# The first unit's probabilities leave PSUM once, as float32, and TensorE multiplies them with the natural values

## The chip, the cores and the metric

The kernel runs on one core of one Trainium2 chip. The metric is the device time of one execution in microseconds (us). The five engines are named as in the profile: PE (TensorE, matrix products; PEld is its weight load), DVE (VectorE), ACT (ScalarE), POOL (GpSimd) and SP (SyncE, which here issues the DMAs). A float32 is exact to 24 bits and a float16 to 11, so this kernel carries most operands as a pair of float16: a high half, and a low half that holds what the high half lost. A product of two such pairs is then three matmuls: high by high, high by low, low by high.

## The reference: clustered attention, then a two-layer network

Inputs: `q`, `k`, `v` of shape (4, 8, 768, 64), that is batch, heads, sequence and head size; 16 centroids per head; weights `w_in` (512 x 2048) and `w_out` (2048 x 512). All are float32.

```python
q_assign = np.argmax(np.einsum('bhsd,hcd->bhsc', q_n, c_n), axis=-1)
k_assign = np.argmax(np.einsum('bhsd,hcd->bhsc', k_n, c_n), axis=-1)
mask = q_assign[:, :, :, None] == k_assign[:, :, None, :]
scores = scale * np.matmul(q, k.transpose(0, 1, 3, 2))
scores = np.where(mask, scores, -1000000000.0)
scores = scores - np.max(scores, axis=-1, keepdims=True)
attn = np.exp(scores)
attn = attn / (np.sum(attn, axis=-1, keepdims=True) + 1e-09)
return np.matmul(attn, v)
```

A query sees only the keys that have the same nearest centroid. The result, as a (3072 x 512) matrix x, goes through `h = x @ w_in`, through a function g (h where h >= 1, 0 where h <= -1, (h + 1)^2 / 4 between), and through `g @ w_out`.

## The kernel before, in words

**Units.** The work is cut into 12 units: four batches (`b`), each in three chunks (`c`) of 256 queries. The heads are taken in four pairs (`hp`). A unit therefore has 16 softmax tiles: four head pairs, two heads (`j`), two tiles of 128 queries (`t`). Each tile is 128 queries by 768 keys.

**One tile.** `at_scores` (lines 891 to 920) multiplies q and k into one of two PSUM pairs (`pair`, two banks each), four matmuls of 384 columns, and DVE copies the scores to an `sS` buffer with their row minimum. `at_soft` (lines 922 to 956) takes the exponential on ACT, with the row sum. The products with v need the probabilities transposed, in `pT`, and there are two ways to that. In all units but the first, ACT writes the high half to an `hl` buffer (three of them), POOL subtracts for the low half, and a DMA transposes both into `pT` (line 955). In the first unit (`by_tensor`, line 958) TensorE transposes six blocks of the float32 probabilities back into the PSUM pair, ACT copies the high half out (line 945), TensorE subtracts that half from the pair with minus the identity `idm` (line 948), and ACT copies what is left, the low half (line 949). In this way the pair is held from the scores to the second copy.

**The products with v.** `at_av` (lines 972 to 1007) spreads the reciprocals of the row sums with 8 small matmuls, then does 36 matmuls per head pair: 6 key blocks, three products of halves, two heads side by side in one bank (`bank_a`). The weights are 64 columns of v, the moving operand 256 columns of `pT`. DVE multiplies the result with the reciprocals into `xn`, and ACT and POOL split it into halves for the network.

**K and V of a head pair** lie in one slot of three parts (`kv_load`, line 668): k arrives in part 1, v in part 2. `k_split` writes the transposed k into part 0. `v_split` (line 709) scales v by a power of two `sv` and writes its halves into part 1, where k had been. `k_assign` finds the clusters of the keys and writes their transposed marks `k1` into part 2, where v had been; so `k1` has to wait for `v_split`, and the scores need `k1`. The scale comes from `v_bound` (line 594, a DVE reduction for each head pair, `v_am` in the profile) and `batch_scale` (line 616), for the whole batch.

**The weights of the network** are scaled and split during the first unit and a part of the second: for each of 16 blocks `w_bits` (ACT and DVE) and `w_split` (two ACT passes, one POOL pass).

**The order of the work** is written by a planner in the kernel (`Recorder`, lines 49 to 322). Each call is recorded with a step number; step 0 is the first score tile, each softmax tile is one step, a unit 16. A model of costs turns the record into one order for each engine, over 80 rounds, and keeps the best; the step numbers are only the first round's priorities. All recorded instructions are issued at line 322, and so nearly every row of the profile has that line. For the first batch `v_split` is entered 6.5 steps ahead of its head pair's first tile (line 1203). A change of the recorded work lets the planner write the whole order anew. Line 102 books a matmul with a float32 moving operand as four times its columns.

Of the kernel before, what the change touches and what calls it, by code (L numbers as in the profile page):

```python
# [24 lines left out]
UNIT = 2.0**-10  # L25
# [394 lines left out]
class Ring:  # L420
# [4 lines left out]

    def __call__(self, *shape, dtype):
        self.i += 1
        return view(self.bufs[self.i % len(self.bufs)], shape, dtype)


def view(buf, shape, dtype):
# [13 lines left out]
def tile_clustered_attention_moe(  # L445
# [33 lines left out]
    PRO = -14  # L479
    FA = SC + LA  # L480
    EARLY = 22
    WA, WR = -4, 2.2

    RAW = [3, 4, 5, 6, 7, 4, 5, 6, 0, 7, 6, 7, 0, 7, 0, None]
# [62 lines left out]
    idb = idf.bitcast(BF16).rearrange("p (q a) -> p q a", a=2)[:, :, 1]  # L547
    idu = const.tile([P, P], F16, name="idu")
    rec.gpsimd.tensor_scalar(out=idu, in0=idf, scalar1=UNIT, scalar2=None, op0=ALU.mult)
    idm = const.tile([P, P], F16, name="idm")  # L550
    rec.gpsimd.tensor_scalar(out=idm, in0=idf, scalar1=-1.0, scalar2=None, op0=ALU.mult)
    iota = const.tile([P, C], F32, name="iota")
    for c in range(C):
        nc.gpsimd.memset(iota[:, c : c + 1], float(C - c))
# [61 lines left out]
    def batch_scale(b):  # L616

        e = BX[b]
        ar = misc(NP + 1)
        rec.tensor.matmul(ar[:, :NP], ones, e["am"], start=True, stop=True)  # L620
        mx = ar[:, NP:]
        isx, sv = new("isx", [1], F32, 3), new("sv", [1], F32, 3)
        rec.vector.tensor_reduce(out=mx, in_=ar[:, :NP], op=ALU.max, axis=AX.X)
        to_scale(mx, sv)
        rec.vector.tensor_copy(isx, mx)
        e.update(isx=isx, sv=sv)

    def transpose(out, nat, ps=None):
        nat = nat.rearrange("p n a d -> p (n a d)")
# [78 lines left out]

    def v_split(b, hp):
        e = KV[b, hp]  # L710
        vs = e["vs"] = view(e["parts"][1], [2, 2, T * D], F16)
        split(vs[:, 0], vs[:, 1], e["v"], BX[b]["sv"])

    def k_assign(b, hp):

        e = KV[b, hp]
        n = 2 * T
        z1 = misc(n, C)
        kn = e["kn"]
        mx = labels(z1, e["kT"], n, [2 * hp + i // T for i in range(n)])  # L720
        rec.vector.tensor_tensor(out=z1, in0=z1, in1=mx, op=ALU.subtract)
        rec.gpsimd.memset(kn[:, :, 1, C:], 0.0)
        rec.vector.tensor_scalar(
            out=kn[:, :, 1, :C], in0=z1, scalar1=0.0, scalar2=-ONE, op0=ALU.not_equal, op1=ALU.mult
        )
        e["k1"] = view(e["parts"][2], [n, P], F16)
        transpose(e["k1"], kn, pair[start()] if b == hp == 0 else None)

        pn = misc(2, C)
        with rec.group():  # L730
            for t in range(T):
                rec.tensor.matmul(pn, ones, kn[:, t::T, 1, :C], start=(t == 0), stop=(t == T - 1))
        rec.vector.tensor_scalar(
            out=BX[b]["has"][:, hp], in0=pn, scalar1=-ONE * (S - 0.5), scalar2=None, op0=ALU.is_gt
        )
# [186 lines left out]
    def at_soft(b, hp, c, j, t):  # L922
        e = A.setdefault((b, hp, c), {})
        n = j * CT + t
        sS, bi, pS = A.pop((b, hp, c, j, t))
        if n == 0:
            e["rs"] = new("rs", [4], F32, 4)
        if t == 0:
            e["pT", j] = new("pT", [2 * T, CT, P], F16, 3)
        sf = sS.rearrange("p a s -> p (a s)")  # L930
        rec.scalar.activation(
            out=sf, in_=sf, func=AF.Exp, bias=bi, scale=-1.0, accum_out=e["rs"][:, n : n + 1]
        )
        pT = e["pT", j]
        if by_tensor(b, hp, c, j, t):
            with rec.group():
                for i in range(T):
                    to = pS[:, i // 3, i % 3 * P : (i % 3 + 1) * P]
                    rec.tensor.matmul(
                        to, sf[:, i * P : (i + 1) * P], idf, start=(i % 3 == 0), stop=False, is_transpose=True,  # L940
                        skip_group_check=True,
                    )
            pt = pS[:, :, :HS].rearrange("p h (n q) -> p h n q", q=P)
            hi, lo = (pT[:, x * T : (x + 1) * T, t, :].rearrange("p (h n) q -> p h n q", h=2) for x in range(2))
            rec.scalar.copy(hi, pt)
            with rec.group():
                for h in range(2):
                    rec.tensor.matmul(pS[:, h, :HS], idm, hi[:, h], start=False, stop=True, skip_group_check=True)
            rec.scalar.copy(lo, pt)
            at_sums(e, n)  # L950
            return
        hl = new("hl", [2, S], F16, 3)
        rec.scalar.copy(hl[:, 0], sf)
        rec.gpsimd.tensor_tensor(out=hl[:, 1], in0=sf, in1=hl[:, 0], op=ALU.subtract)
        rec.sync.dma_start_transpose(out=pT[:, :, t, :], in_=hl.rearrange("p a s -> p (a s)"))
        at_sums(e, n)

    def by_tensor(b, hp, c, j, t):

        return early() and b == c == 0  # L960

    def at_sums(e, n):
        if n == 3:
# [8 lines left out]
    def at_av(b, hp, c):  # L972
        u = b * NCH + c
        e, kv = A.pop((b, hp, c)), KV[b, hp]

        pv, rb = bank_a[:, :CQ], bank_a[:, CQ:]
        with rec.group():
            for t in range(CT):
                for a in range(2):
                    for j in range(2):  # L980
                        n = j * CT + t
                        rec.tensor.matmul(
                            rb[j * D : (j + 1) * D, t * P : (t + 1) * P],
                            e["rr"][:, a, n : n + 1].to_broadcast([P, D]),
                            idu,
                            start=(a == 0),
                            stop=(a == 1),
                        )
            for kc in range(T):
                for i, (va, pa) in enumerate(((0, 0), (0, 1), (1, 0))):  # L990
                    for j in range(2):
                        pT = e["pT", j].rearrange("p (a n) t q -> p a n (t q)", a=2)[:, pa, kc]
                        rec.tensor.matmul(
                            pv[j * D : (j + 1) * D],
                            kv["vs"][:, va, j, kc * D : (kc + 1) * D],
                            pT,
                            start=(kc == 0 and i == 0),
                            stop=(kc == T - 1 and i == 2),
                        )
        rs = new("rb", [CQ], F32)  # L1000
        rec.scalar.copy(rs, rb)
        xn = rs
        rec.vector.tensor_tensor(out=xn, in0=pv, in1=rs, op=ALU.mult)
        if hp == 0:
            X[u] = new("x", [2, NP, CQ], F16)
        rec.scalar.copy(X[u][:, 0, hp], xn)
        rec.gpsimd.tensor_tensor(out=X[u][:, 1, hp], in0=xn, in1=X[u][:, 0, hp], op=ALU.subtract)
# [190 lines left out]
    for b in range(B):  # L1198
        for hp in range(NP):
            s0 = first(b, hp, 0)  # L1200

            if b == 0:
                steps = [PRO, s0 - 9, s0 - 8, s0 - 6.5, s0 - 6]
            else:
                steps = [first(b - 1, hp, NCH - 1) + SC + LA - 3] + [s0 - x for x in (6, 5.6, 5, 4)]
            for x, fn in zip(steps, (kv_load, k_scale, k_split, v_split, k_assign)):
# [74 lines left out]
```

## Time and profile before

| | |
|---|---|
| timed runs, median of 3 | 872.43 us (872.41 to 873.12) |
| profiled execution, span from first to last instruction | 870.7 us |
| PE busy | 812.9 us (93%) |
| DVE busy | 647.3 us (74%) |
| ACT busy | 650.3 us (75%) |
| POOL busy | 546.3 us (63%) |
| mean granted clock of PE | 0.983 |

The span is the time that the profile shows of the profiled execution; what lies around it is not in the trace, and the median of the timed runs is 1.7 us above it. The engines' shares are means over the whole span. The first 180 us or so differ from the rest, and so the profile has to be read by stages. In a row of a group stand the line, the engine, the operation, output <- inputs, the shapes and the count; then busy time and the mean of one in ns; then idle time of the engine just before, and what ended it.

### The profile page before, as it was taken

Reading aid. Unit: us, or ns where it says so; the run is one execution under the profiler, and the core shown is the slowest. Engines: PE = TensorE matmul, PEld = TensorE weight load, DVE = VectorE, ACT = ScalarE, POOL = GpSimd, SP = SyncE. Lnnn points to the kernel's source line nnn. Section 1 sums busy time; section 2 is a strip of 40 time slices with the busy share of each in tenths; the row PEclk is TensorE's granted clock in tenths of the full one; section 3 lists DMA queues with packets and bytes.
Section 4 is the critical chain, followed back from the end, with each engine's and each line's share of the span. In section 5 each row is a group of like instructions: output and inputs, shape, how many; then the busy total and the mean of one; then the engine's idle time right before and its main releaser. Section 6 shows DMA issues by size and latency. Waiting matters only on the chain.

```text
span 870.7 us, 19881 instructions
## 1 busy us (share of the span) xinstructions
PE 812.9 (93%) x7532; PEld 566.1 (65%) x7532; DVE 647.3 (74%) x1535; ACT 650.3 (75%) x1144; POOL 546.3 (63%) x528
## 2 busy tenths in 40 slices
PE   3677768999999999999999999999999999999998
PEld 3454546667667767767767766767766666766664
DVE  7999999989878777668789848867687758444322
ACT  6999998798777688777767777787777787776232
POOL 1245499797655768756757677766757667766222
PEclk9888899999999999999999999999999999999999
DMA  9956689779999979989999969989898797766100
GB/s 315 241 180 164 164 206 200 140 123 194 169 186 197 183 146 179 190 152 164 195 177 188 176 126 178 188 158 179 168 202 178 145 174 127 127 116 110 20 25 25
DMA packets 404193, 141.01 MB, mean 162 GB/s; under 512 B 372736, under 2 KB 396288, under 8 KB 404096
## 3 DMA queue, kind: packets, MB, share of 16 engines
q1 hardware_dynamic: 404096, 139.73, 81.2%
q8 instruction: 59, 0.97, 0.5%
q14 instruction: 38, 0.31, 0.1%
HBM read 40.40 MB, written 6.29 MB: 54 GB/s over the span
## 4 chain that ended last, share of the span: by engine, by line
PE 76%; DVE 10%; ACT 7%; issue 3%; POOL 2%; DMA 2%; SPq 0%; ACTq 0%; POOLq 0%; DVEq 0%
PE pair L322 37%; PE banka L322 11%; PE bankh L322 9%; PE banki L322 9%; PE bankj L322 9%; POOL hl L322 2%; DVE sS L322 2%; ACT sS L322 1%; ACT w L322 1%; DVE w L322 1%; ACT pT L322 1%; DVE r L322 1%; DVE qn L322 1%; DMA kv<-in_v_dram 1%; ACT hl L322 1%
## 5 line engine op out<-in xcount | busy, mean ns | idle before, releaser
L322 POOL TENSOR_TENSOR hl<-sS,hl 128x768 f16<-128x768 f32 x176 | 298.9, 1703 | 111.5 <-ACT hl L322 86.7
L322 PE MATMUL pair<-w,g 128*128 128x512 f16 x1152 | 271.1, 379 | 0.3 <-ACT o L322 0.3
L322 PEld LDWEIGHTS <-w 128*128 128x128 f16 x2304 | 223.2, 98 | 48.6 <-issue 7.1
L322 ACT ACTIVATE sS<-sS,sbi 128x768 f32<-128x768 f32 x192 | 179.4, 934 | 85.7 <-DVE sbi L322 75.7
L322 DVE CUSTOM_DVE_ANT_0 sS<-pair,zero,er 128x768 f32<-128x768 f32 x192 | 194.1, 1011 | 61.4 <-PE pair L322 47.7
L322 PEld LDWEIGHTS <-g 128*128 128x128 f16 x1152 | 110.2, 98 | 116.1 <-issue 2.9
L322 PE MATMUL pair<-kv,q 128*128 128x384 f16 x768 | 159.1, 331 | 20.2 <-ACT pT L322 9.1
L322 POOL TENSOR_TENSOR g<-r,g 128x512 f16<-128x512 f32 x88 | 106.0, 1204 | 72.2 <-ACT g L322 68.5
L322 ACT CAST hl<-sS 128x768 f16<-128x768 f32 x176 | 144.1, 827 | 4.3 <-DMA pT<-hl 2.5
L322 PEld LDWEIGHTS <-q 128*128 128x128 f16 x1152 | 83.9, 98 | 76.3 <-issue 28.9
L322 PEld LDWEIGHTS <-kv 128*64 128x64 f16 (+1 forms) x2112 | 104.5, 108 | 5.8 <-issue 1.9
L322 ACT ACTIVATE r<-r,f_ra,f_rs 128x512 f32<-128x512 f32 x88 | 71.5, 812 | 45.3 <-DVE r L322 42.8
L322 PE MATMUL banka<-pT,kv 128*64 128x256 f16 x1728 | 103.6, 274 | 1.7 <-DMA pT<-hl 1.7
L322 ACT CAST g<-r 128x512 f16<-128x512 f32 x88 | 53.7, 610 | 10.9 <-DVE r L322 5.6
L322 PE MATMUL bankj<-x,w 128*128 128x256 f16 x432 | 51.7, 272 | 0.3 <-DVE r L322 0.2
L322 PE MATMUL bankh<-x,w 128*128 128x256 f16 x408 | 48.8, 273 | 2.4 <-POOL x L322 2.3
L322 POOL TENSOR_TENSOR qn<-qn,phi 128x256 f16<-128x256 f16 x48 | 32.4, 692 | 20.5 <-DVE phi L322 18.4
L322 POOL TENSOR_TENSOR w<-w 128x1024 f16<-128x1024 f32 x12 | 27.4, 2282 | 23.8 <-ACT w L322 23.8
L322 PE MATMUL banki<-x,w 128*128 128x256 f16 x312 | 37.7, 273 | 0.6 <-DVE w_iw L322 0.6
L322 PE MATMUL banki<-wk,w 128*128 128x256 f16 x312 | 37.0, 273 | 0.1
L322 DVE TENSOR_SCALAR r<-bankh,f_lo,f_hi 128x512 f32<-128x512 f32 x29 | 23.4, 808 | 17.8 <-PE bankh L322 16.5
L322 ACT ACTIVATION_READ_ACCUMULATOR sS<-sS,sbi 128x1 f32 x192 | 36.2, 189 | 0.0
(232 smaller groups left out, 1082.8 us busy)
## 6 DMA issues: line engine op xcount, KB each, us to landing
w<-in_moe_w_out_dram SPq DMA_DIRECT2D x14, 512.0 KB, 4.4
q<-in_q_dram SPq DMA_DIRECT2D x12, 512.0 KB, 5.0
kv<-in_k_dram SPq DMA_DIRECT2D x16, 384.0 KB, 4.0
kv<-in_v_dram SPq DMA_DIRECT2D x16, 384.0 KB, 4.6
out_dram<-o SPq DMA_DIRECT2D x11, 512.0 KB, 3.4
w<-in_moe_w_in_dram SPq DMA_DIRECT2D x10, 512.0 KB, 6.0
word<-in_moe_w_in_dram SPq DMA_DIRECT2D x6, 512.0 KB, 4.5
o<-in_v_dram SPq DMA_DIRECT2D x8, 384.0 KB, 3.8
```

The lines of the kernel that those rows point to most:

```text
L322: fn(*args, **kw)
```

## The change: what it does

Only the first unit (`b == c == 0`) and the first batch's v are touched.

1. The six transposes of a tile stay. ACT then copies the whole tile out of PSUM once, as float32, scaled by 2^-10 (`UNIT`), into the same `pT` buffer seen as float32. The subtracting matmuls, the second copy and the constant `idm` go.
2. In `at_av` the first unit does 12 matmuls of float32 per head pair: the natural v as weights, the float32 probabilities moving. The multiplication into `xn` takes a further factor, `sv1` (the scale `sv` by 2^10), a new 128x1 value of `batch_scale`.
3. For the first batch `k1` goes to part 1 (where k had been) and v stays in part 2. `v_split` is entered at step `s0 + 16` instead of `s0 - 6.5`: it writes its halves into an `hl` buffer, and a DMA on SP's queue copies them over v in part 2. The later units of the batch read them there.

```diff
+    VL = 9
...
-    idm = const.tile([P, P], F16, name="idm")
-    rec.gpsimd.tensor_scalar(out=idm, in0=idf, scalar1=-1.0, scalar2=None, op0=ALU.mult)
...
+        if b == 0:
+            e["sv1"] = const.tile([P, 1], F32, name="sv1")
+            rec.vector.tensor_scalar(out=e["sv1"], in0=sv, scalar1=1 / UNIT, scalar2=None, op0=ALU.mult)
...
-        vs = e["vs"] = view(e["parts"][1], [2, 2, T * D], F16)
+        to = e["vs"] = view(e["parts"][2 if b == 0 else 1], [2, 2, T * D], F16)
+        vs = new("hl", [2, 2, T * D], F16, 3) if b == 0 else to
         split(vs[:, 0], vs[:, 1], e["v"], BX[b]["sv"])
+        if b == 0:
+            rec.sync.dma_start(to, vs)
...
-        e["k1"] = view(e["parts"][2], [n, P], F16)
+        e["k1"] = view(e["parts"][1 if b == 0 else 2], [n, P], F16)
...
+            if whole(b, c):
+                e["pT", j] = view(rings["pT"].last(), [T, CT, P], F32)
...
-        if by_tensor(b, hp, c, j, t):
+        if whole(b, c):
             with rec.group():
                 for i in range(T):
                     to = pS[:, i // 3, i % 3 * P : (i % 3 + 1) * P]
-                    rec.tensor.matmul(
-                        to, sf[:, i * P : (i + 1) * P], idf, start=(i % 3 == 0), stop=False, is_transpose=True,
-                        skip_group_check=True,
-                    )
-            pt = pS[:, :, :HS].rearrange("p h (n q) -> p h n q", q=P)
-            hi, lo = (pT[:, x * T : (x + 1) * T, t, :].rearrange("p (h n) q -> p h n q", h=2) for x in range(2))
-            rec.scalar.copy(hi, pt)
-            with rec.group():
-                for h in range(2):
-                    rec.tensor.matmul(pS[:, h, :HS], idm, hi[:, h], start=False, stop=True, skip_group_check=True)
-            rec.scalar.copy(lo, pt)
+                    rec.tensor.transpose(to, sf[:, i * P : (i + 1) * P], idf)
+            rec.scalar.activation(
+                out=pT[:, :, t, :].rearrange("p (h n) q -> p h n q", h=2),
+                in_=pS[:, :, :HS].rearrange("p h (n q) -> p h n q", q=P),
+                func=AF.Copy,
+                scale=UNIT,
+            )
             at_sums(e, n)
             return
...
-    def by_tensor(b, hp, c, j, t):
+    def whole(b, c):
 
-        return early() and b == c == 0
+        return b == c == 0
...
-            for kc in range(T):
+            for kc in range(T if whole(b, c) else 0):
+                for j in range(2):
+                    rec.tensor.matmul(
+                        pv[j * D : (j + 1) * D],
+                        kv["v"][:, j, kc * D : (kc + 1) * D],
+                        e["pT", j][:, kc].rearrange("p t q -> p (t q)"),
+                        start=(kc == 0),
+                        stop=(kc == T - 1),
+                    )
+            for kc in range(0 if whole(b, c) else T):
...
+        if whole(b, c):
+            rec.vector.scalar_tensor_tensor(
+                out=xn, in0=pv, scalar=BX[b]["sv1"], in1=rs, op0=ALU.mult, op1=ALU.mult
+            )
...
-                steps = [PRO, s0 - 9, s0 - 8, s0 - 6.5, s0 - 6]
+                steps = [PRO, s0 - 9, s0 - 8, s0 + LA + VL, s0 - 6]
```

More of the change, by code (lines that the diff above doesn't have):

```diff
@@ L427, in __call__, with last @@
         self.i += 1
-        return view(self.bufs[self.i % len(self.bufs)], shape, dtype)
+        return view(self.last(), shape, dtype)
+    def last(self):
+        return self.bufs[self.i % len(self.bufs)]
 def view(buf, shape, dtype):
@@ L1002, in at_av @@
         xn = rs
-        rec.vector.tensor_tensor(out=xn, in0=pv, in1=rs, op=ALU.mult)
+        if whole(b, c):
+            rec.vector.scalar_tensor_tensor(
+                out=xn, in0=pv, scalar=BX[b]["sv1"], in1=rs, op0=ALU.mult, op1=ALU.mult
+            )
+        else:
+            rec.vector.tensor_tensor(out=xn, in0=pv, in1=rs, op=ALU.mult)
         if hp == 0:
```

## The prediction

> **What bounds the kernel now.** I first read the busy time of each engine stage by stage. The cuts are the first unit's first score matmul (24.39 us), the end of that unit's softmax (106.6), and points where the picture changes.
>
> ```profile
> span 870.7 us, 19881 instructions
> ...
> core 0: us, PE busy (x) PEld busy (x) DVE busy (x) ACT busy (x) POOL busy (x), PEclk, DMA share, GB/s
> 0.00:24.39 24.39, 8.55 (x118) 7.36 (x119) 19.11 (x61) 16.79 (x28) 3.68 (x28) 1.00 0.95 311
> 24.39:106.60 82.21, 59.01 (x545) 41.21 (x547) 76.64 (x212) 77.34 (x116) 33.43 (x32) 0.83 0.73 189
> 106.60:140.00 33.40, 23.45 (x225) 16.46 (x220) 32.91 (x73) 32.72 (x53) 32.25 (x20) 1.00 0.83 183
> 140.00:190.00 50.00, 46.73 (x441) 33.18 (x440) 44.30 (x120) 41.36 (x78) 44.36 (x39) 1.00 0.82 156
> 190.00:850.00 660.00, 658.83 (x6114) 458.10 (x6113) 469.66 (x1069) 476.55 (x865) 429.07 (x408) 1.00 0.85 157
> ```
>
> From 190 us on TensorE is busy 658.83 of 660 us: that part is a fixed quantity of matmul work, and it only moves as a block. The time is therefore decided before 190 us, and the change touches only that part. In the first unit TensorE has 82.21 - 59.01 = 23.2 us free, while VectorE (DVE) is busy 76.64 and ScalarE (ACT) 77.34 of 82.21: both at 93 to 94%. From 106.6 to 140 both are full, and GpSimd (POOL) too. So a stretch before 140 us is shortened by what comes off DVE and ACT together, or by their gaps closing; one of them alone is not enough.
>
> Then the chain of waits, by line, in the first two stretches (first row 0 to 24.39, second 24.39 to 106.6):
>
> ```profile
> by line: DMA q<-in_q_dram 18.9%; DVE v_am L322 14.1%; DVE n L322 9.0%; DVE qn L322 7.1%; DVE mx L322 5.8%; issue 5.7%; DVE bankh L322 5.5%; DVE aq L322 5.0%; DVE w L322 4.6%; DVE banki L322 4.5%; DVE wk L322 2.5%; ACT qn L322 2.1%; SPq L322
> ```
>
> ```profile
> by line: PE pair L322 12.7%; ACT pT L322 12.3%; DVE w L322 10.1%; issue 9.2%; ACT w L322 8.9%; DVE sS L322 7.5%; ACT sS L322 7.0%; ACT wk L322 5.4%; PE banka L322 4.3%; DVE wk L322 4.0%; PE bankh L322 2.3%; DVE qn L322 2.0%; ACT x L322 1.5%
> ```
>
> Before the first scores the chain runs through DVE, 14.1% of it in the reductions over v. In the first unit it hops between all engines, and no line holds over 13%: the copies out of PSUM (ACT pT) are one link of many.
>
> **What is removed.** The groups of the first unit, engine by engine:
>
> ```profile
> L322 PE MATMUL pair<-kv,q 128*128 128x384 f16 x72 | 17.6, 378 | 12.6 <-ACT pT L322 9.1 <-DVE q L322 2.0 <-DVE rs L322 1.3
> L322 PE MATMUL pair<-idf,sS 128*128 128x128 f32 x96 | 16.1, 313 | 7.1 <-ACT sS L322 6.5
> L322 PE MATMUL pair<-pT,idm 128*128 128x384 f16 x32 | 9.7, 391 | 1.7 <-ACT pT L322 1.7
> L322 PE MATMUL banka<-pT,kv 128*64 128x256 f16 x108 | 7.4, 300 | 0.0
> ```
>
> ```profile
> L322 ACT CAST pT<-pair 128x768 f16<-128x768 f32 x32 | 24.6, 790 | 1.9 <-PE pair L322 1.9
> L322 ACT ACTIVATE sS<-sS,sbi 128x768 f32<-128x768 f32 x16 | 15.0, 936 | 1.0 <-DVE sbi L322 1.0
> ...
> L322 ACT ACTIVATE kv<-kv,sv 128x768 f16<-128x768 f32 x3 | 2.8, 948 | 0.0
> ```
>
> ```profile
> L322 DVE CUSTOM_DVE_ANT_0 sS<-pair,zero,er 128x768 f32<-128x768 f32 x17 | 17.2, 1013 | 3.9 <-PE pair L322 3.4 <-ACT sS L322 0.3 <-ACT rb L322 0.2
> ...
> L322 DVE SCALAR_TENSOR_TENSOR kv<-kv,sv 128x768 f16<-128x768 f32 x3 | 3.0, 1008 | 0.0
> ```
>
> The 16 second copies leave ACT: 16 x 24.6/32 = 12.3 us. The one copy that stays writes float32 instead of float16 from the same 768 elements; no row has that form, so I bound it by 0.77 (same time) and by twice that, and take 0.77, since the exp rows that write 768 float32 take 0.94 with two column operands. The 32 subtracting matmuls leave TensorE: 9.7 us, all of it in a stretch where TensorE has 23.2 us free, so their own worth is zero. What they and the second copy do besides is hold the PSUM pair: score matmuls stand idle 9.1 us for ACT pT, and DVE in turn 3.4 us for those scores.
>
> **The products with v.** 36 float16 matmuls per head pair become 12 on float32 (the 8 that spread 1/sum stay). The same-shaped rows, at full and at lower clock:
>
> ```profile
> 50.26 2.13 PE L322 MATMUL banka<-pT,kv 128*64 128x256 f16 x36
> ...
> 88.64 3.18 PE L322 MATMUL banka<-pT,kv 128*64 128x256 f16 x36
> ```
>
> No row shows a float32 product that is not a transpose. Lower bound: the float32 transposes cost 16.1/96 = 0.168 us each against 0.129 for bfloat16 ones of the same size,
>
> ```profile
> L322 PE MATMUL pair<-idf,n 128*128 128x128 bf16 x24 | 3.1, 306 | 1.1 <-DVE n L322 1.1
> ```
>
> a factor 1.3, so 12 x 2.13/36 x 1.3 = 0.9 us. Upper bound: four half-precision products each, and the two heads no longer side by side (now 36 matmuls of 273 to 300 ns fit in 2.13 us because they overlap): 48 x 2.13/36 x 2 = 5.7 us. I take four products, still side by side: 2.8 us; the planner books a float32 operand the same way (line 103, n times 4; a booking, no measurement). The four head pairs then cost 4 x (2.8 - 2.1) = +2.8 us of TensorE, between -5 and +14; net with the 9.7 removed -6.9, between -15 and +4.7. All within 23.2 us of free time. Without that cover the upper end would add its 4.7 us.
>
> [...]
>
> **What moves: the split of v.** Its four pairs of instructions (ACT 0.95, DVE 1.0 each) leave the time ahead of the first unit's products. k1 no longer overwrites v, so it stops waiting for them. The reductions over v and the batch scale stay, but are now due at the first products (50 us) instead of before the first scores:
>
> ```profile
> 10.11 0.95 DVE L322 TENSOR_REDUCE v_am<-kv 128x1 bf16<-128x768 f32 x1
> ...
> 11.89 2.67 DVE L322 TENSOR_REDUCE v_am<-kv 128x1 bf16<-128x768 f32 x3
> ...
> 16.27 0.16 DVE L322 RECIPROCAL sv<-bankj 128x1 f32<-128x1 f32 x1
> ...
> 20.24 1.00 DVE L322 SCALAR_TENSOR_TENSOR kv<-kv,sv 128x768 f16<-128x768 f32 x1
> ```
>
> 3.5 us of reductions and 1.0 of split can so step out of the way of the first scores. But DVE has no free time behind it: the 3.5 us only change places. The splits do leave: DVE up to 106.6 loses 4 x 1.0 = 4.0 us. They come back at steps 16, 20, 24 and 28, due at the second unit's products. The first two fall into the stretch 106.6 to 140, where DVE has 33.40 - 32.91 = 0.5 us free, and cost their 2.0 us there. The last two I put behind 140, where TensorE already holds 46.73 of 50 us and DVE has 5.7 us free: nothing.
>
> New with them are four DMAs from an hl buffer to the kv slot, on the SP queue between the transposing DMAs of the second unit. Rows to size them:
>
> ```profile
> x<-in_v_dram SPq DMA_DIRECT2D x2, 384.0 KB, 3.7
> pT<-hl SPq DMA_TRANSPOSE x12, 4.1
> ```
>
> ```profile
> L322 POOL TENSOR_TENSOR hl<-sS,hl 128x768 f16<-128x768 f32 x176 | 298.9, 1703 | 111.5 <-ACT hl L322 86.7
> ...
> L322 ACT CAST hl<-sS 128x768 f16<-128x768 f32 x176 | 144.1, 827 | 4.3 <-DMA pT<-hl 2.5
> ```
>
> A softmax tile holds an hl buffer for 0.8 + 1.7 + 4.1 = 6.6 us, a late split for 0.95 + 1.0 + 3.7 = 5.7. Sixteen tiles and four splits over three buffers need (16 x 6.6 + 4 x 5.7)/3 = 42.8 us, and the second unit takes about 53 (106.6 to 160). So I book them at 0, with an upper bound of 4 x 5.7/3 = 7.6 us if the buffers have no slack. The copy waits on SP for DVE's low half; queued behind it are the transposes, and for these the second unit's products wait. The copy's source is on chip; no row shows such a copy, and I price it as the load.
>
> Small ones: one more 128x1 on DVE (0.16 us), a scalar column in four multiplications; together 0.4 us.
>
> **The sum.** DVE gaps that close in the first unit: of its 5.6 us I take the 3.4 that waited for the pair, since second copy and subtraction sat in that loop. -3.4 (gaps) - 4.0 (splits out) + 2.0 (two of them back on a full DVE) + 0.4 (small) = -5.0 us. ACT loses 12.3 + 3.7 in all and is no longer at the limit; it adds nothing beyond the gaps, because DVE stays at its limit. Against the span: 870.7 - 5.0 = 865.7. The median of the timed runs is 872.43, 1.7 over the span; with the same surround the forecast is 867.4 us. What is late next is DVE, at some 97%.
>
> **The rivals.** *DVE alone sets the pace.* The gaps don't close (they belong to the order of the work) and all four splits come back on full engines: 0 - 4.0 + 4.0 + 0.4, 872.8 us. For it: DVE at 93% before and 99% from 106.6 to 140. Against: 3.4 of its idle time names the pair.
>
> *The pair's turn-round sets the pace.* Eight rounds of two tiles take 82.21 us, 10.3 each; a round loses one subtraction (0.5) and one copy (0.79), 8 x 1.3 = 10.3 us, if the weights' work on DVE can all slip past the unit: 862.1 us. For it: 9.1 us of idle scores behind ACT pT. Against: that weights' work is due soon after, on engines that are full.
>
> *Slower: the late splits choke the hl ring in the second unit.* Place: 106.6 to 160. The buffers have no slack, the full 7.6 us falls due, and all splits find DVE full, 2.0 more; with the gain of 5.0 this makes +4.6, 877.0 us. It decides as soon as tiles wait for hl buffers. For it: three transposes in 8.62 us already fill the queue there,
>
> ```profile
> 111.43 8.62 SPq L322 DMA_TRANSPOSE pT<-hl  x3
> ```
>
> and POOL sits in the chain with them. Against: ACT's idle for DMA pT<-hl is only 2.5 us in the whole run, by the row above.
>
> *The clock drops.* The first unit already runs at 0.83, with stretches far lower:
>
> ```profile
> 30.00:40.00 10.00, 7.12 (x39) 4.60 (x39) 9.12 (x33) 9.30 (x14) 3.26 (x2) 0.69 0.98 256
> ...
> 50.00:60.00 10.00, 7.38 (x102) 5.72 (x100) 9.76 (x32) 9.93 (x15) 2.71 (x2) 1.00 0.90 247
> ...
> 80.00:90.00 10.00, 7.86 (x48) 5.21 (x49) 8.35 (x20) 8.30 (x13) 6.86 (x9) 0.53 0.63 214
> ```
>
> With 9.7 us of matmuls gone TensorE may look idle more often. At 0.6 instead of 0.83, its remaining 52 us become 72 of 77: scores and transposes arrive later by what the copy saved, the gaps stay open, and two splits come back: -2.0 + 0.4 + some 1 of queueing, 871.8 us, no change. [...]
>
> **How the numbers follow.** Forecast 0.47, DVE alone 0.18, clock 0.05, turn-round 0.13, hl ring 0.17. A measurement here tells 0.2% (1.7 us) from no change. Faster: 0.47 + 0.13 = 0.60; same: 0.23; slower: 0.17. The forecast's own range, with its terms between their bounds, is 863 to 870.6. The whole range goes from 861 (turn-round, a little past) to 875.5 (most of the way to the choked ring).
>
> **What would show it.** Right: ACT pT x16 in the first unit; 12 float32 products near 2.8 us per head pair; DVE over 95% up to the unit's end; that end near 100 us instead of 106.6; ACT clearly under DVE; the TensorE-full part starting some 5 us earlier. Wrong: products near 5.7 us with scores waiting behind them, idle time on ACT or DVE for hl buffers between 105 and 155 us, or a first unit that ends early while the full part starts as late as now.

## The result, and the profile after

| | before | after |
|---|---|---|
| timed runs, median of 4 each | 872.7 us (872.41 to 873.12) | 879.33 us (878.01 to 880.3) |
| ratio, 95% interval | | 1.0087 (1.0068 to 1.0106) |
| profiled execution, span | 870.7 us | 878.5 us |
| PE busy | 812.9 us | 814.5 us |
| DVE busy | 647.3 us | 662.1 us |
| ACT busy | 650.3 us | 639.6 us |

The changed kernel is 0.9% slower; the forecast was 867.4 us, in a range of 861 to 875.5. From the top of the page of after:

```profile
span 878.5 us, 19683 instructions
...
PE 814.5 (93%) x7452; PEld 563.1 (64%) x7452; DVE 662.1 (75%) x1536; ACT 639.6 (73%) x1128; POOL 542.7 (62%) x527
```

By the cuts of the prediction, the windows of after (columns as before):

```profile
24.39:106.60 82.21, 58.35 (x504) 38.27 (x503) 79.13 (x218) 70.57 (x106) 38.38 (x35) 0.83 0.78 212
106.60:140.00 33.40, 25.50 (x211) 18.66 (x211) 32.27 (x63) 28.66 (x47) 27.51 (x19) 0.90 0.73 177
140.00:190.00 50.00, 45.41 (x421) 31.15 (x421) 48.96 (x126) 40.57 (x75) 40.89 (x34) 1.00 0.82 151
190.00:850.00 660.00, 651.98 (x6038) 451.43 (x6037) 475.40 (x1063) 474.39 (x863) 427.02 (x408) 1.00 0.85 157
```

The last row is the surprise. Before, TensorE was busy 658.83 of these 660 us; after, 651.98. The change adds no work there and takes none away.

**One way to read the whole loss.** Split the span at 200 us: span = 200 + (TensorE's busy time still to come at 200 us) + (TensorE's idle time after 200 us). The first term says how far the beginning got, the second how well the rest runs. The time to come is the page's PE total less the first two windows; the idle time is what is left of the span. Windows of before, then of after:

```profile
0.00:106.60 106.60, 67.56 (x663) 48.57 (x665) 95.74 (x271) 94.13 (x143) 37.11 (x60) 0.87 0.78 217
106.60:200.00 93.40, 80.18 (x753) 56.11 (x748) 87.07 (x210) 82.61 (x145) 84.26 (x62) 1.00 0.84 166
200.00:800.00 600.00, 598.83 (x5649) 417.60 (x5649) 444.62 (x1027) 451.37 (x823) 407.26 (x389) 1.00 0.90 167
```

```profile
0.00:106.60 106.60, 67.62 (x627) 46.46 (x628) 98.67 (x279) 88.33 (x134) 41.51 (x62) 0.87 0.80 232
106.60:200.00 93.40, 80.90 (x729) 56.91 (x729) 90.49 (x207) 77.65 (x137) 75.19 (x60) 0.96 0.77 158
200.00:800.00 600.00, 591.98 (x5547) 410.34 (x5545) 449.14 (x1018) 445.76 (x815) 402.85 (x386) 1.00 0.90 167
```

- Before: 812.9 - 67.56 - 80.18 = 665.2 us to come, and 870.7 - 200 - 665.2 = 5.5 us idle.
- After: 814.5 - 67.62 - 80.90 = 666.0 us to come, and 878.5 - 200 - 666.0 = 12.5 us idle.

So of the 7.8 us of span, 0.8 is a beginning that is not ahead at all, and 7.0 is new idle time after 200 us. The waits of PE from 190 to 850 us (columns: engine, buffer and line that waited, what for, us in total, times, longest), before and then after:

```profile
PE pair L322 <- DVE sbi L322: 0.7, 1, 0.7
PE bankj L322 <- DVE r L322: 0.2, 1, 0.2
```

```profile
PE pair L322 <- DVE sbi L322: 3.5, 8, 0.8
PE bankj L322 <- DVE r L322: 1.9, 1, 1.9
PE bankj L322 <- DMA q<-qn: 0.8, 1, 0.8
PE banka L322 <- DMA pT<-hl: 0.6, 1, 0.6
PE bankh L322 <- DVE zs L322: 0.6, 1, 0.6
PE bankj L322 <- DMA kv<-n: 0.4, 1, 0.4
```

Most of the new waits are for DVE: eight short ones for the copy of the scores with their minimum, one for the network's function g, and one more. 1.8 us are waits for DMAs. They are spread over the units; the window of 20 us that holds the longest of them, before and then after:

```profile
240.00:260.00 20.00, 20.00 (x191) 13.94 (x189) 15.68 (x41) 15.39 (x29) 11.79 (x12) 1.00 0.94 184
```

```profile
240.00:260.00 20.00, 18.03 (x143) 11.90 (x142) 12.98 (x34) 13.79 (x25) 12.04 (x11) 0.91 0.87 169
```

**What the first unit did.** PE's timeline (start, duration), before, then after. The `banka<-idu,rr` matmuls open the products of a head pair: here the fourth of the first unit and the first of the second.

```profile
106.37 0.41 PE L322 MATMUL banka<-idu,rr 128*64 128x128 f16 x8
...
123.70 0.41 PE L322 MATMUL banka<-idu,rr 128*64 128x128 f16 x8
```

```profile
47.63 2.76 PE L322 MATMUL banka<-pT,kv 128*64 128x256 f32 x24
...
99.95 0.64 PE L322 MATMUL banka<-idu,rr 128*64 128x128 f16 x8
100.38 3.40 PE L322 MATMUL banka<-pT,kv 128*64 128x256 f32 x24
131.62 0.41 PE L322 MATMUL banka<-idu,rr 128*64 128x128 f16 x8
```

The first unit ends 6.4 us earlier, as forecast, and the second unit's first products come 7.9 us later. Between the two lie 17.3 us before and 31.7 after: the planner has put other work there (from 100 to 131.6 us DVE is busy 30.33 of 31.60 us). This is the last sign of being wrong that the prediction named: a first unit that ends early, and a full part that starts no earlier. The order of every engine is new, not only that of the first unit.

### The profile page after: what moved, and what is told of

Same layout as the page of the kernel before. It is cut to its first block, busy times and chain, and to the rows that moved or that the text cites. A ratio compares the mean times of both kernels' runs of the same rounds, so it can differ in the third digit from the quotient of the medians.

```text
span 878.5 us, 19683 instructions
## 1 busy us (share of the span) xinstructions
PE 814.5 (93%) x7452; PEld 563.1 (64%) x7452; DVE 662.1 (75%) x1536; ACT 639.6 (73%) x1128; POOL 542.7 (62%) x527
## 4 chain that ended last, share of the span: by engine, by line
PE 62%; DVE 12%; issue 4%; POOL 3%; ACT 3%; DMA 2%; ACTq 0%; DVEq 0%; POOLq 0%
PE pair L322 30%; PE banka L322 9%; PE banki L322 8%; PE bankj L322 7%; PE bankh L322 7%; DVE sS L322 3%; DVE r L322 2%; POOL hl L322 2%; DVE bankh L322 1%; DVE qn L322 1%; DVE bankj L322 1%; DMA pT<-hl 1%; DVE q L322 1%; DMA kv<-n 1%; DMA q<-qn 1%
## 5 line engine op out<-in xcount | busy, mean ns | idle before, releaser
L322 POOL TENSOR_TENSOR hl<-sS,hl 128x768 f16<-128x768 f32 x176 | 297.3, 1696 | 121.2 <-ACT hl L322 93.7
L322 DVE CUSTOM_DVE_ANT_0 sS<-pair,zero,er 128x768 f32<-128x768 f32 x192 | 194.1, 1011 | 51.4 <-PE pair L322 39.8
L322 PE MATMUL pair<-kv,q 128*128 128x384 f16 x768 | 162.0, 335 | 20.3 <-DVE sbi L322 10.0
L322 PE MATMUL banka<-pT,kv 128*64 128x256 f16 (+1 forms) x1680 | 105.7, 280 | 0.6 <-DMA pT<-hl 0.6
L322 PEld LDWEIGHTS <-kv 128*64 128x64 f16 (+1 forms) x1968 | 96.1, 107 | 3.9 <-issue 1.1
L322 POOL TENSOR_TENSOR qn<-qn,phi 128x256 f16<-128x256 f16 x48 | 30.2, 648 | 25.7 <-DVE phi L322 25.7
L322 DVE SCALAR_TENSOR_TENSOR qn<-q,sq,qn 128x256 f16<-128x256 f32 x48 | 34.2, 744 | 2.7 <-ACT qn L322 2.5
```

Of the source, the lines that this page charges most:

```text
L322: fn(*args, **kw)
```

## The experiments

Three questions were asked in turn: is it the changed work or the new order; is it a part of the change, or DVE; and what do other orders of both kernels give. "To come" and "idle" below are the two terms at 200 us, from each run's own profile, as above.

**1. Work and order apart.** The planner's search is replaced by a list of node numbers (all recorded instructions then have line 313 in the profile, and 321 in the kernels of experiment 5), and so the changed work runs in the order of before (instructions that only one kernel has are put where their dependences allow), and the old work in the order of after.

```diff
-        for _ in range(ROUNDS):
...
-        span, self.order = best
+        self.order = [self.nodes[i] for i in unpack(ORDER)]
```

> The changed work, issued in the order that the planner wrote for the kernel before: every instruction that both have keeps its place, the subtractions and second copies are dropped, and each late split goes ahead of the exponential of the second unit's first tile of its head pair. Theory 'order' (the loss of 6.6 us comes from the order that the planner drew anew): 866 to 872 us, not slower than before, TensorE idle after 190 us near 1 us as before. Rival 'work' (the late splits, their copies and the float32 products cost the time themselves): 876 us or more, with the hl buffers or DVE named in the waits between 105 and 190 us.

> The work of before, issued in the order that the planner wrote for the changed kernel; subtraction and second copy follow the first copy, the splits of v stand ahead of k's cluster marks. 'Order': 876 to 883 us, with several us of TensorE idle after 190 us. 'Work': 870 to 875 us.

Measured: e1 891.5 us, ratio 1.0225 (1.0209 to 1.0241); e2 924.86 us, 1.0609 (1.059 to 1.0628). Both mixtures are far slower than either kernel. e1 lies where 'work' expected it, e2 beyond both expectations. But an order fits the work for which it was written, so this pair cannot share the loss out between work and order. It does show how much order alone can cost: e2 holds the work of before unchanged and loses 6%. In e1 the loss lies before 200 us (683.5 us to come, 6.2 idle). ACT's timeline, then the waits from 104 to 180 us:

```profile
126.61 0.83 ACT L313 CAST hl<-sS 128x768 f16<-128x768 f32 x1 [6.20 <-DMA pT<-hl]
```

```profile
ACT hl L313 <- DMA pT<-hl: 14.6, 4, 6.2
PE pair L313 <- DVE sbi L313: 8.4, 9, 2.3
PE bankj L313 <- DVE wk L313: 8.2, 1, 8.2
```

The late splits hold hl buffers, and the second unit's tiles wait for them: the prediction's slower rival, in an order that left no room for the splits. The 8.4 us are hardly new (6.9 in before, over the same stretch); the one wait of 8.2 us for the weights' work on DVE is, and e9, without the splits, has 0.5 us of it.

**2. The late splits.** Both keep the float32 products and leave out the late splits of the first batch's v with their DMAs; its later units read what lies in another part of the slot. e9 has the order of before, e10 that of after.

```diff
     def v_split(b, hp):
+        if b == 0:
+            e["vs"] = view(e["parts"][0], [2, 2, T * D], F16)
+            return
```

> The kernel of the first experiment (changed work in the order of before, 891.5 us) with the four late splits and their copies left out; the later units of the first batch multiply with the halves of k in their place, so the output is not the reference's. Theory 'hl': the late splits choke the hl buffers and the SP queue between 104 and 180 us, and that made 891: 866 to 874 us, and ACT's 14.6 us of waiting for DMA pT<-hl in that stretch shrink to under 4. Rival 'order': the order of before cannot use the saving whatever is left out: 882 us or more.

> After, in its own order as it stands (not planned anew), with the four late splits and their copies left out in the same way. 'hl': the second unit's first products (131.6 us) come forward by 6 us or more, and the time falls to 868 to 873. Rival 'DVE': VectorE, full from 86 to 135 us with the weights' passes, holds the second unit; the products come forward by at most 3 us, and the time falls by the splits' own 4 to 6 us of DVE, to 873 to 876.

Measured: e9 869.51 us, 0.9977 (0.9959 to 0.9995), 661.7 to come and 6.1 idle; e10 878.71 us, 1.0094 (1.0068 to 1.0121), 664.0 and 13.7. In the order of before the splits were worth 22 us (e1 against e9), and without them the changed work puts TensorE 3.5 us ahead at 200 us. (That is more than the float32 products alone: the second copies and subtractions are gone, and the first batch's v is not split at all.) e9 came out as 'hl' expected. e10 met neither expectation: the second unit's first products come 3.6 us earlier (128.06 us), and the time stays, as does the idle time after 200 us. In the kernel's own order the splits thus cost nothing that the timed runs show, and this speaks against the hl-ring rival for the pair that was compared; nor do ACT's waits in after, from 90 to 200 us, name a DMA from hl. e10 from 200 us on:

```profile
200.00:800.00 600.00, 590.69 (x5506) 408.33 (x5504) 449.07 (x1016) 443.22 (x812) 401.04 (x386) 1.00 0.89 167
```

**3. Is DVE the bound?** One of DVE's passes over 15 of the 16 blocks of the network's weights is left out (the one that puts the signs back, so that these weights lose their signs), in each kernel's own order.

```diff
         if part is None:
-            rec.vector.scalar_tensor_tensor(
-                out=lo, in0=hi, scalar=0x80000000, in1=lo, op0=ALU.bitwise_and, op1=ALU.bitwise_or
-            )
```

> After, in its own order, without the DVE pass that puts the sign on 15 weight blocks (1.3 us each, 19 us of VectorE, nearly all before 150 us); the weights lose their signs, so the output is not the reference's. 'DVE': it is the bound from the first scores to 150 us: the second unit's first products come 6 us or more before 131.6, and the time falls by 8 to 14 us, to 865 to 871. 'hl': these products stay within 3 us of 131.6, the time falls by less than 5.

> Before, in its own order, without the same pass. 'DVE': ACT is as full as DVE here, so less comes of it than in the changed kernel: the time falls by 3 to 8 us, to 864 to 869, and the changed kernel's fall is larger by 3 us or more. 'hl': both fall alike, by less than 5.

Measured: e11 873.57 us, 1.0021 (1.0001 to 1.0041), 658.6 to come and 13.4 idle; e12 872.29 us, 1.0018 (1.0005 to 1.0032), 663.3 and 6.3. In before, DVE is busy 632.8 instead of 647.3 us, 14.5 less and nearly all of it before 200 us, and the span falls by 1.1; against the kernel before in the same session the timed runs show no gain. So DVE alone, busy 93 to 99% up to 140 us, was not the bound there. ACT stays full. The first unit in e12 (columns as in the prediction):

```profile
24.39:106.60 82.21, 57.78 (x573) 40.81 (x575) 68.88 (x214) 79.18 (x120) 33.81 (x34) 0.90 0.75 190
```

DVE is down to 84% of it and ACT stands at 96%. That is what the prediction had said of this kernel: DVE and ACT together, one alone is not enough. In after, where ACT has room (busy 70.57 of 82.21 us in the first unit), DVE is busy 645.8 instead of 662.1, 16.3 less, and the span falls by 6.5, all of it in the first 200 us: there DVE's time has a price, though not one to one. e11 lies between its two expectations, and e12 under what 'DVE' expected. The idle time after 200 us does not fall, but the pass hardly runs there (DVE 448.13 us from 200 to 800, against 449.14), so this says nothing of DVE's part in the later waits.

**4. Do DVE and POOL hold each other up?** Some rows of DVE in after are much longer than others of the same shape (2.95 and 1.01 us, 1.53 and 0.16). DVE's timeline, then POOL's:

```profile
31.53 0.16 DVE L322 SCALAR_TENSOR_TENSOR bankh<-ik,iq 128x1 f32<-128x1 f32 x1
...
93.78 2.95 DVE L322 SCALAR_TENSOR_TENSOR hl<-kv,sv,hl 128x768 f16<-128x768 f32 x1
...
116.38 1.01 DVE L322 SCALAR_TENSOR_TENSOR hl<-kv,sv,hl 128x768 f16<-128x768 f32 x1
...
242.15 1.53 DVE L322 SCALAR_TENSOR_TENSOR bankh<-ik,iq 128x1 f32<-128x1 f32 x1
```

```profile
93.78 2.14 POOL L322 TENSOR_TENSOR w<-w 128x1024 f16<-128x1024 f32 x1 [0.54 <-ACT w L322]
...
117.18 1.72 POOL L322 TENSOR_TENSOR hl<-sS,hl 128x768 f16<-128x768 f32 x1 [4.97 <-ACT hl L322]
...
242.01 1.64 POOL L322 TENSOR_TENSOR hl<-sS,hl 128x768 f16<-128x768 f32 x1 [2.73 <-ACT hl L322]
```

The operation on one column took 1.53 us beside a POOL subtraction, and ended when that did; 0.16 at 31.53, where POOL runs nothing from 28 to 34 us. The late split took 2.95 us beside one of 2.14, and 1.01 at 116.38, where POOL stood idle until 117.18. The 1.53 us at 242.15 stands right ahead of the operation whose result PE waits 1.9 us for. Not every operation of DVE is held in this way: a copy of the scores took 1.01 us at 117.77, inside POOL's subtraction from 117.18 to 118.90, and the mean of all 192 in after is 1011 ns. What sets the ones that are held apart was not tested.

To take this away, POOL's subtraction (which reads) becomes two fills with zero (which read nothing), 747 ns each in e13 where the subtraction took 1696; the low half of the probabilities is left out in all units but the first.

```diff
-        rec.gpsimd.tensor_tensor(out=hl[:, 1], in0=sf, in1=hl[:, 0], op=ALU.subtract)
+        for _ in range(2):
+            rec.gpsimd.memset(hl[:, 1], 0.0)
```

> After, in its own order, with the 176 subtractions on POOL that make the low half of a probability tile replaced by two writes of zeros into the same half (about as long, nothing read; the low half is then zero, a part of the precision is left out). Theory 'collision' (DVE operations on on-chip memory stand still while POOL's tensor operation runs, and the three orders differ in how often that happens): DVE's busy time falls from 662 to under 645, TensorE's idle time from 200 to 800 us from 8.0 to under 3, the time by 6 us or more, to 865 to 873. Rival 'sequence' (what comes before what on each engine makes the idle time): idle stays at 6 or more, the time falls by less than 3.

> Before, in its own order, with the same replacement. 'Collision': DVE's busy time falls from 647 to near the same level as the other two (within 5 us), the time by 0 to 3 us, since this order has few collisions that count. 'Sequence': the time falls by less than 3 here too, and the distance of 7 us to after stays.

> Before in its second round's order (882.5 us), with the same replacement. 'Collision': DVE's busy time falls from 668 to within 5 us of the other two, the time by 8 us or more, to 868 to 874; the three orders end within 4 us of each other. 'Sequence': 878 or more.

Measured: e13 871.63 us, 1.001 (0.9992 to 1.0028), 659.6 to come and 9.9 idle; e14 871.12 us, 1.0001 (0.9984 to 1.0019), 663.8 and 5.2; e15 (the order of e3, below) 881.94 us, 1.0123 (1.0087 to 1.016), 675.5 and 4.7. One group of DVE shows fewer collisions, after and then e13 (another, `q<-q,phi`, does not: 516 ns in after, 601 in e13); the fills of e13 follow:

```profile
L322 DVE SCALAR_TENSOR_TENSOR qn<-q,sq,qn 128x256 f16<-128x256 f32 x48 | 34.2, 744 | 2.7 <-ACT qn L322 2.5
```

```profile
L313 DVE SCALAR_TENSOR_TENSOR qn<-q,sq,qn 128x256 f16<-128x256 f32 x48 | 23.5, 521 | 2.8 <-ACT qn L313 2.7
...
L313 POOL MEMSET hl<- 128x768 f16 x352 | 260.0, 747 | 34.5 <-DMA pT<-hl 24.4
```

Without the subtraction the ratio of after falls from 1.0087 to 1.001, and that of before stays at 1. The span of after falls by 9.0 us: 6.4 of it are gained before 200 us, and of the 7.0 us of new idle time only 2.6 go. The slow order of before (e15 against e3) is hardly helped: 0.5 us, in two timed runs. The edit also loads POOL less (501.1 us busy instead of 542.7) and frees the score buffers a little sooner, so even these 9.0 us are the collisions' upper end. They are a part of this order's trouble; they are not what makes the order of e3 slow. e13 meets 'collision' in DVE's time and in the span, but not in the idle time from 200 to 800 us (5.4, where under 3 was expected); e15 came out as 'sequence' expected.

**5. Other orders of both kernels.** The planner keeps the best by its own booked time of 80 rounds. Here the second, third, fourth and fifth best are issued instead, work unchanged.

```diff
-            if best is None or span < best[0]:
-                best = span, self.order
+            ranked.append((span, len(ranked), self.order))
...
-        span, self.order = best
+        span, _, self.order = sorted(ranked)[1]
```

> Before, with the second best of the planner's 80 rounds in place of the best; the planner books it 0.6 us longer (869.3 against 868.7). 'Order': the booking says little, so anywhere from 871 to 880 us, and more than 2 us from 872.7 would show it. 'Work': 871 to 875 us, since nothing of the work is changed.

> After, with the second best of its 80 rounds, booked 0.1 us longer (871.2 against 871.1). 'Order': more than 2 us away from 879.3, as low as 870. 'Work': 877 to 882 us, as after.

> Before with its third best round (booked 871.9). Theory 'draw': the orders of before scatter over some 10 us, the best round was a lucky one, and the two sets of orders overlap: 874 to 886 us, with the middle of before's four orders no lower than that of after's four. Rival 'work': the changed work adds about 6 us to whatever order: before's third and fourth at 870 to 876, after's at 878 to 884.

> Before with its fourth best round (booked 872.2). 'Draw': 874 to 886 us. 'Work': 870 to 876 us.

> After with its third best round (booked 872.8). 'Draw': 870 to 884 us. 'Work': 878 to 884 us.

> After with its fourth best round (booked 874.2). 'Draw': 870 to 884 us; if the first unit's saving of some 5 us is real in each order, after's four lie lower in the middle than before's four. 'Work': 878 to 884 us.

> After with its third round once more, to narrow the interval. 'Draw' (the changed work is some 3 us cheaper than the old in the mean of the orders): 0.1 to 0.4% faster than before, with an interval below 1. 'Work': not faster.

> The kernel before with the fifth-best booked of its 80 orders, kept as a test of a reading made from the other orders: span = 200 + TensorE's busy time that is left at 200 us + its idle time after 200 us. The four orders of the kernel before have 665.2, 674.5, 671.5 and 666.5 us left at 200 us (mean 669.4) and 5.5, 7.0, 7.1 and 7.3 us of idle after it. Theory that the changed work puts TensorE ahead in the first 200 us on average, and that the order adds a scatter: 666 to 674 left, idle 5 to 8, median 873 to 883, at or above the time before. Rival, that the two kernels scatter alike about one mean: as likely under 664 left as over 669, median anywhere from 869 to 882.

> The changed kernel with the fifth-best booked of its 80 orders. Its four orders have 666.0, 662.8, 661.6 and 663.7 us left at 200 us (mean 663.5), and 12.5, 11.3, 7.1 and 6.2 us of idle after it. Theory that the changed work puts TensorE ahead by about 6 us at 200 us whatever the order: 661 to 666 left, clearly under the kernel before in its own fifth order; idle after 200 us anywhere from 6 to 13, median 869 to 880. Rival, that the two kernels scatter alike about one mean: as likely over 668 left as under 664.

Measured; the last two columns are the starts of the first unit's last products and of the second unit's first:

| order | median us | ratio (interval) | to come | idle | unit 1 last | unit 2 first |
|---|---|---|---|---|---|---|
| before, best | 872.7 | 1 | 665.2 | 5.5 | 106.4 | 123.7 |
| before, 2nd (e3) | 882.45 | 1.0131 (1.0101 to 1.0161) | 674.5 | 7.0 | 111.3 | 130.7 |
| before, 3rd (e5) | 879.39 | 1.0078 (1.0061 to 1.0095) | 671.5 | 7.1 | 116.0 | 133.7 |
| before, 4th (e6) | 877.8 | 1.0065 (1.0041 to 1.009) | 666.5 | 7.3 | 109.7 | 128.6 |
| before, 5th (e17) | 878.16 | 1.0069 (1.0046 to 1.0093) | 669.1 | 7.6 | 115.2 | 132.7 |
| after, best | 879.33 | 1.0087 (1.0068 to 1.0106) | 666.0 | 12.5 | 100.0 | 131.6 |
| after, 2nd (e4) | 876.87 | 1.0064 (1.0044 to 1.0085) | 662.8 | 11.3 | 100.0 | 128.8 |
| after, 3rd (e7) | 871.26 | 0.9989 (0.9976 to 1.0001) | 661.6 | 7.1 | 100.0 | 127.2 |
| after, 4th (e8) | 873.8 | 1.0029 (1.0005 to 1.0052) | 663.7 | 6.2 | 100.9 | 126.8 |
| after, 5th (e18) | 878.51 | 1.0072 (1.0048 to 1.0097) | 668.0 | 10.3 | 102.6 | 127.1 |
| mean, before | 878.1 | | 669.4 | 6.9 | 111.7 | 129.9 |
| mean, after | 876.0 | | 664.4 | 9.5 | 100.7 | 128.3 |

Three things follow. First, one and the same work runs in 872 to 882 us (before) or 871 to 879 us (after), by its order alone. The 6.6 us between the two kernels are within what another order of either does. Second, the pair that was compared is an unlucky one for the change. The order of before is the best of its five in both terms; that of after has the most idle time of its five and the second most to come. Over five orders each the changed kernel is 2.1 us faster, but with standard deviations of 3.5 and 3.4 us that difference has a standard error of 2.2: not established. (The five are the best booked of each search, not drawn at random, so the standard errors here are a rough guide; and the two terms come from one execution each.) Third, the two terms part. At 200 us the changed kernel is ahead by 4.9 us (standard error 2.0), and afterwards it idles 2.6 us more (1.3). e18 missed its expectation (668.0 to come, where 661 to 666 was expected), and so the lead is likely, not sure. Of the others, e3 came out above all that was expected of it (882.45), e4 as 'order' and e5 to e8 as 'draw' expected, and e17 within both of its readings.

e16 repeats e7's order: 871.34 us, 0.9995 (0.9979 to 1.0012). This missed the 0.1 to 0.4% gain that 'draw' expected: that order is no faster than the kernel before by any interval here; of the versions run, only e9, which leaves work out, is below it by its whole interval.

## Why the prediction was wrong, point by point

**Two steps failed**, one for each term. The sum put the beginning 5.0 us ahead and the rest at +0; the pair shows +0.8 and +7.0. So 7.0 us of the miss lie behind 200 us and 5.8 before it.

*The rest.* The prediction read that the part from 190 us on "is a fixed quantity of matmul work, and it only moves as a block". What was left at 200 us is nearly the same (665.2 and 666.0 us), but TensorE does not stay full while it is done. The text before the prediction had said that a change of the recorded work lets the planner write the whole order anew, and neither the sum nor a rival gave that a price. The changed work does not force the loss: in its third-best order (e7) it idles 7.1 us after 200 and takes 871.26 us. Nor does a rival of the prediction carry the 7.0: it stands in e10 and in e11 as well (13.7 and 13.4 us idle), without late splits and without a DVE pass. Its size goes with the order, 5.5 to 12.5 us over the ten; three of the changed kernel's five orders lie above all five of before, so a part may belong to the changed work, and no run separates that.

*The beginning.* The sum took DVE's durations from the order of before; by its terms DVE's work grows by 0.4 us in all, since the splits of v that leave come back. In after DVE is busy 14.8 us longer (662.1 against 647.3), 6.4 of it before 200 us. Without POOL's subtraction this difference is gone. Before (e14), then after (e13):

```profile
PE 813.9 (94%) x7532; PEld 567.1 (65%) x7532; DVE 637.6 (73%) x1535; ACT 650.9 (75%) x1144; POOL 502.4 (58%) x704
PE 808.9 (93%) x7452; PEld 560.5 (64%) x7452; DVE 637.0 (73%) x1536; ACT 639.5 (74%) x1128; POOL 501.1 (58%) x703
```

And then the changed kernel is 4.2 us ahead at 200 us (659.6 to come against 663.8), near the 5.0 of the sum; it still idles 4.7 us more afterwards (9.9 against 5.2). So in this order the gain of the beginning was there, and DVE's longer operations beside POOL's subtraction (662.1 us busy, 637.0 without it) took it back, as far as one execution of each can show.

**The float32 products** were right: 2.76 us in three of the four head pairs, at a granted clock of 0.99 to 1.00, where 2.8 was taken (3.40 in the fourth, at a granted clock of 0.79 from 100 to 104 us), the two heads still side by side (the bounds were 0.9 and 5.7). The profile shows 24 records for the 12 matmuls that the kernel issues, and those of the first head pair start in twos, 4 to 5 ns apart. The factor of four rested on the planner's booking, with which 48 times 2.13/36 us make an estimate of 2.84; the runs show the 2.76 us, and not how TensorE comes to it.

**The copy** was right. ACT's row in after, from 15 to 130 us:

```profile
L322 ACT ACTIVATE pT<-pair 128x768 f32<-128x768 f32 x16 | 12.7, 793 | 0.5 <-PE pair L322 0.5
```

793 ns where 0.77 us was taken, and 16 of them.

**The first unit's end** was right in the pair: 100.0, forecast "near 100". Over five orders each it comes 11.0 us earlier (111.7 against 100.7), close to the 10.3 of the turn-round rival. Whether that rival had the reason was not tested, and it too failed behind the first unit: the second unit's first products come only 1.6 us earlier on average. The gap between the two units has grown by 9.4 us and holds other work; 4.9 us of lead are left on average at 200 us.

**DVE and ACT** went as said in their shares of the first unit's stretch: DVE 79.13 of 82.21 us (96%), ACT 70.57. DVE's idle time there fell from 5.6 to 3.1 us, 2.5 of the 3.4 that were taken. What a microsecond of DVE is worth was taken too high. The sum booked three of its terms (-4.0, +2.0, +0.4) one to one; e11 took 16.3 us off DVE in the changed kernel, and TensorE had 7.4 us less to come at 200 us. The "DVE alone" rival has e12 against it: 14.5 us off DVE in the kernel before, and no gain while ACT stayed full.

**The reductions over v** did not step aside. DVE's timeline in after, and PE's first scores:

```profile
9.71 0.94 DVE L322 TENSOR_REDUCE v_am<-kv 128x1 bf16<-128x768 f32 x1
...
11.49 2.67 DVE L322 TENSOR_REDUCE v_am<-kv 128x1 bf16<-128x768 f32 x3
```

```profile
24.47 2.50 PE L322 MATMUL pair<-kv,q 128*128 128x384 f16 x8
```

They stay ahead of the first scores (24.47 us, 24.39 before). A later due time is a permission, not a move.

**The late splits' cost** of 0 held in the kernel's own order (e10), with its upper bound of 7.6 us far too low for an order that does not expect them (e1 against e9: 22 us). DVE's half of a split took 1.5 us on average instead of 1.0 (the row of 2.95 us above is one), and the first runs at 93.78 us, ahead of the first unit's end. Their DMA is cheaper than taken, 2.8 us to land instead of 3.7:

```profile
kv<-hl SPq DMA_DIRECT2D x4, 384.0 KB, 2.8
```

**The clock** rival had nothing to do in the first unit: 0.83 before and after. That a TensorE with less to do is granted a lower clock is not shown: in the prediction's windows of 10 us of before it was busy 7.12 us at 0.69, 7.38 at 1.00 and 7.86 at 0.53. From 106.6 to 140 us the granted clock was 0.90 instead of 1.00; TensorE had 7.9 us free there, and whether that cost anything is not shown.

**The range** ended at 875.5 since every case in it took the order as given. The kernel before alone, in five orders, covers 10 us.

**What stays open.** What makes one order slow: the slow orders of before lose it before 200 us (e3: 9.3 us more to come than the best), the slow ones of after partly behind it. The collisions explain at most the 9.0 us of e13, and next to nothing of e3; nor does DVE's busy time rank the orders (660.1 us in e8 at 873.8, 648.6 in e17 at 878.16). And whether the changed work is faster in its best possible order was not found: the best one run equals the kernel before.

## What to carry to other kernels

Where a planner or a heuristic writes the order from the recorded work, an edit has two effects: its own cost, and a new draw of the order. Measure the second first, by issuing a few other orders of the unchanged kernel; here they scatter by 10 us, twice what the edit was meant to bring, and the booked time doesn't rank them. Then compare several orders of each version, with the span split at the point behind which the work is the same: how much is left there, and how much idles afterwards. And test "this engine is the bound" by taking work off it before summing its times, with an eye on which engine is full next to it.

## What the runs showed of the hardware that was not expected

**Some DVE operations took far longer beside a subtraction on POOL.** 1.53 us instead of 0.16 for one column, 2.95 instead of 1.01 for 768 (rows above). The copies of the scores did not: 1011 ns in the mean in before, in after and in e13. With 176 subtractions of 1.7 us on POOL there is much to meet: the 48 operations `qn` took 34.2 us in after, 26.7 in before and 23.5 in e13. The row before, in the kernel before:

```profile
L322 DVE SCALAR_TENSOR_TENSOR qn<-q,sq,qn 128x256 f16<-128x256 f32 x48 | 26.7, 598 | 4.0 <-ACT qn L322 4.0
```

A mean duration of such a group is then a property of the order too, and a term of a sum taken from it moves when the order does.

**In two executions, a lower clock before 200 us was paid from idle time.** e7 and e16 are the same kernel; their windows up to 200 us, e7 and then e16:

```profile
0.00:106.60 106.60, 68.55 (x631) 47.35 (x632) 98.19 (x284) 86.98 (x134) 40.92 (x62) 0.87 0.76 225
106.60:200.00 93.40, 84.08 (x766) 58.41 (x767) 89.09 (x207) 80.42 (x138) 84.80 (x62) 0.95 0.86 175
```

```profile
0.00:106.60 106.60, 66.50 (x631) 46.15 (x632) 97.95 (x284) 87.15 (x134) 43.36 (x62) 0.90 0.78 226
106.60:200.00 93.40, 81.31 (x774) 57.32 (x775) 89.35 (x207) 80.39 (x138) 84.60 (x62) 1.00 0.85 175
```

TensorE is busy 152.6 and 147.8 us, at clocks of 0.87 and 0.95 against 0.90 and 1.00. With TensorE's totals of 814.2 and 809.3 us, 661.6 and 661.5 us are to come, and the medians are 871.26 and 871.34 us. Of these two executions, the one at the lower clock had TensorE 4.8 us busier before 200 us and as much less idle, and the time stayed. It is also why "to come at 200 us" is the better measure of the beginning than its busy or idle time.
